# An attention-plus-two-MoE kernel: shorter first warm-up, v sums on GpSimd, pooled normalising in halves, another choice of engine, and the first batch's two outputs added in PSUM

## The chip, the cores and the metric

The kernel runs on one core of a Trainium2 chip. The metric is the device time of one execution in microseconds; lower is better.

## The reference

For 4 batches of 8 heads, 576 positions and head size 64, two attentions are added. The first works on q, k and v averaged over groups of four positions (144 x 144 scores), and each of its rows is repeated four times. The second is local: each position sees those less than four away. The sum, as a matrix x of 2304 tokens by 512, goes through two feed-forward layers of width 2048.

```
out_up    = repeat(softmax(q_d k_d^T / 8) v_d, 4)     # *_d: mean over 4 positions
out_local = softmax(masked(q k^T / 8)) v              # |i - j| < 4
x = out_up + out_local
h = x @ w_in;   x = (h * sigmoid(h)) @ w_out
h = x @ w_in2;  g = (a0 + a1 h + a2 h^2 + a3 h^3) / (1 + |b0||h| + |b1| h^2 + 1e-6)
out = g @ w_out2
```

## The kernel before

**Precision.** Each MoE operand is split into a high part (rounded to the fast float32 form) and a low rest, and each product is three matmuls: high by high, high by low, low by high. `xh`/`xl` are the parts of x, `gh`/`gl` those of the activated h, and the weights are split by `piece` (seven jobs for each piece of 128 columns, on ACT, DVE and GpSimd).

**Stages.** The first layer's tokens go in five blocks of 5, 5, 5, 5 and 4 chunks of 96 tokens (`BLOCKS1`), and each block goes over 16 slices of the width. A step is one slice of one block: 12 matmuls of L807 into a bank `hps` (tag "h", two buffers), `th` and `sg` on ACT and DVE, then `gh` and `gl`, then 12 matmuls of L821. Block 0 does slices 0 to 7, then block 1 all 16, then block 0 its rest. Block 0 needs chunks 0 to 4 of batch 0; block 1 needs chunk 5 of batch 0 and chunks 0 to 3 of batch 1. The second layer (L1054 and others) has a fixed order and is not touched.

**Attention.** Of each batch, the pooled part runs in two rounds m: scores (job s, L471), maximum (m), exponentials (e, ACT), sums (u), normalising (n, L496), transposes for each half e_ (t0, t1, L505), copies (c0, c1), product with v's sums (o, L519), and copy to `up` (U). The sums of v over four positions are jobs p (L424 on DVE, L426 and L427 on GpSimd) in batch 0, and accumulating loads in the others. The local part goes chunk by chunk: S (L572, L581), M, E, U, N (L606), T (L617), C, O (product, L637), A (the addition of the upsampled result from PSUM, L644, into `xs`, two buffers), H (copy to `xh`) and X (L659, subtraction to `xl`). PSUM tiles of attention come from the ring "pair": one buffer, and two of "acc" that are lent to it until the first MoE step.

**Order.** A planner (`Plan`) lists the jobs with costs in ns on engines P (PE), V (DVE), A (ACT), G (GpSimd) and D (the SP queue's loads), simulates them by due time and resources, and emits the instructions in the order it finds. That order is fixed from then on: an engine waits at each instruction for what it needs. A job with `port=True` may go to GpSimd or DVE, and the planner lets only one such job run at a time.

**Warm-up.** `warm(n)` issues n dummy matmuls (L289) into a tile `wps`, which has the tag "h" as well. There are 20 at the start. In the head, wherever the plan has PE idle before a job, more are put in:

```
    warm(WARM0)
    busy = 0.0
    for x in order:
        if x.eng == "P":
            if busy < HEAD + 15000:
                warm(int((x.start - busy) * WARM_SHARE / 109))
            busy = x.end
        x.emit(x.eng)
```

with HEAD = 34000 and WARM_SHARE = 0.8, times in planned ns.

Of the kernel before, what the change touches and what calls it, by code (L numbers as in the profile page):

```python
# [49 lines left out]
PATIENCE = 900.0  # L50
BACKLOG = 4000.0
EARLY = 50000.0
ROUNDS = 6
WARM0 = 20
WARM_SHARE = 0.8


W_LOW = 2.0 ** -15
# [35 lines left out]
class Plan:  # L94
# [27 lines left out]
    def run(self, when):  # L122
# [26 lines left out]
        while events:  # L149
            t = heapq.heappop(events)  # L150
            while events and events[0] <= t:
                heapq.heappop(events)
            while done and done[0][0] <= t:
                _, _, j = heapq.heappop(done)
                for u in j.give:
                    u.left -= 1
                    if u.left == 0:
                        self.rings[u.home].append(u.no)
                for x in users.get(id(j), ()):
                    x.wait -= 1  # L160
                    lat = (0.0 if j.eng == "P" else self.OWN) if j.eng == x.only() else self.LAT
                    x.ready = max(x.ready, t + lat + x.margin)
                    if x.wait == 0:
                        pool.append(x)
                        heapq.heappush(events, x.ready)
            pool.sort(key=lambda j: j.t)
            again = True
            while again:
                again = False
                for j in pool:  # L170
                    if j.ready > t:
                        continue
                    if j.t - j.early > t:
                        heapq.heappush(events, j.t - j.early)
                        continue
                    need = {}
                    for u in j.take:
                        need[u.ring] = need.get(u.ring, 0) + 1
                    if any(len(self.rings[r]) + len(self.rings[self.lent[r]] if r in self.lent else ()) < k
                           for r, k in need.items()):  # L180
                        continue

                    best = next(iter(j.cost))
                    if best == "D" and bus > t + BACKLOG:
                        heapq.heappush(events, bus - BACKLOG)
                        continue
                    if free[best] > t and not (j.port and "G" in j.cost):
                        if free[best] <= t + PATIENCE:
                            continue
                        best = next((e for e in j.cost if free[e] <= t), None)  # L190
                        if best is None:
                            continue
                    if "G" in j.cost and "V" in j.cost and j.port:
                        best = next((e for e in "VG" if free[e] <= t), None)
                        if best is None:
                            continue
                    held = best == "G" or (best == "V" and j.port)
                    if held and port > t:
                        heapq.heappush(events, port)
                        continue  # L200
                    for u in j.take:
                        u.home = u.ring if self.rings[u.ring] else self.lent[u.ring]
                        u.no = self.rings[u.home].pop(0)
                    if j.closes:
                        self.lent.clear()
                    j.eng, j.start = best, t
                    free[best] = t + j.cost[best]
                    if held and not (best == "G" and j.size):
                        port = free[best]
                    heapq.heappush(events, free[best])  # L210
                    if j.size:
                        bus = max(bus, free[best]) + j.size / self.DMA_RATE
                        j.end = bus + self.DMA_LAT
                    else:
                        j.end = free[best]
                    n += 1
                    heapq.heappush(done, (j.end, n, j))
                    heapq.heappush(events, j.end)
                    order.append(j)
                    pool.remove(j)  # L220
                    again = True
                    break
# [32 lines left out]
def tile_kernel(ctx, tc, kq, kqs, vp, vw_in, moe_w_in, moe_w_out, moe2_w_in, moe2_w_out, moe2_a, moe2_b, out):  # L255
# [67 lines left out]
    def eng(e):  # L323
        return {"V": nc.vector, "G": nc.gpsimd}[e]
# [50 lines left out]
    def attention(b):  # L375
# [22 lines left out]
        if b == 0:  # L398
# [12 lines left out]
            for i in range(2):  # L411
                for hf in range(2):
                    wn = 2 * i + hf + NF - 7
                    u = Unit(f"w{wn}")
                    st = {}
                    def lv(e, i=i, hf=hf, st=st, wn=wn):
                        st[0] = wp.tile([128, 4, 256], F32, tag=f"w{wn}", name="vst")[:HS]
                        nc.sync.dma_start(out=st[0], in_=vp[b, :, :, i, 256 * hf:256 * hf + 256].rearrange("r s c -> s r c"))
                    def pv(e, i=i, hf=hf, st=st):
                        if not vdt:  # L420
                            vdt[0] = at.tile([HS, 2, DM], F32, tag="vd", name="vd", bufs=1)
                        o = vdt[0][:, i, 256 * hf:256 * hf + 256]
                        if e == "V":
                            nc.vector.tensor_reduce(out=o, in_=st[0].rearrange("p r c -> p c r"), axis=AX.X, op=ALU.add)  # L424
                        else:
                            nc.gpsimd.tensor_tensor(out=st[0][:, 0:2], in0=st[0][:, 0:2], in1=st[0][:, 2:4], op=ALU.add)  # L426
                            nc.gpsimd.tensor_tensor(out=o, in0=st[0][:, 0], in1=st[0][:, 1], op=ALU.add)  # L427
                    l = plan.add(f"v{b}{i}{hf}", FAR, {"D": 60}, lv, take=[u], size=HS * 4096)
                    vs.append(plan.add(f"p{b}{i}{hf}", FAR, {"G": 2050, "V": 1950}, pv,
                                       after=[l] + vs[:1], take=[] if vs else [vdu], give=[u]))  # L430
        else:
            def ks(e, r):
# [27 lines left out]
        for m in range(2):  # L460
# [31 lines left out]
                nc.vector.tensor_reduce(out=x["r"], in_=x["e"], axis=AX.X, op=ALU.add)  # L492
                nc.vector.reciprocal(out=x["r"], in_=x["r"])

            def no(e, x=x):
                eng(e).tensor_tensor(out=x["e"][:, :, :SD], in0=x["e"][:, :, :SD],  # L496
                                     in1=x["r"].unsqueeze(2).to_broadcast([128, 6, SD]), op=ALU.mult)

            def tr(e, x=x, e_=0, u=None):
                x["t", e_] = pair(u)  # L500
# [28 lines left out]
            jm = plan.add(f"m{b}{m}", d0, {"V": v_ns(864)}, mx, after=[js])  # L529
            je = plan.add(f"e{b}{m}", d0, {"A": 6 * (a_ns(SD) + 93) + 200}, ex, after=[jm], give=[p0])  # L530
            ju = plan.add(f"u{b}{m}", d0, {"V": v_ns(870) + 200}, su, after=[je])
            jn = plan.add(f"n{b}{m}", d0, {"V": v_ns(864), "G": 130 + 1.9 * 864}, no, after=[ju], port=True)
            pc, pt_ = [], []
            for e_, u in ((0, p1_), (1, p2)):
                jt = plan.add(f"t{b}{m}{e_}", d0, {"P": 500}, lambda e, tr=tr, e_=e_, u=u: tr(e, e_=e_, u=u),
                              after=[jn] + pt_[:1], take=[u] + ([pt] if e_ == 0 else []), give=[eu], margin=MARGIN if b else MARGIN0)
                pt_.append(jt)
                pc.append(plan.add(f"c{b}{m}{e_}", d0, {"A": a_ns(576), "V": v_ns(576)},
                                   lambda e, tc_=tc_, e_=e_: tc_(e, e_=e_), after=[jt] + pc[:1], give=[u]))
# [6 lines left out]
        for c in range(NCH):  # L546
# [79 lines left out]
                    x["p"] = at.tile([128, 2, 4 * SUB], F32, tag="PT", name="PT", bufs=3)  # L626
                copy(e, x["p"], x["t"][:, :, :4 * SUB])

            def pv(e, x=x, pO=pO):
                op = x["o"] = pair(pO)  # L630
                for m in range(2):
                    for s_ in range(2):
                        for e_ in range(2):
                            for a in range(2):
# [1 line left out]
                                o = SUB * (2 * e_ + m)  # L636
                                nc.tensor.matmul(op[64 * e_:64 * e_ + 64, a, CH * m + SUB * s_:CH * m + SUB * s_ + SUB],  # L637
                                                 lhsT=x["v"][r, s_, 2 * m + e_, :], rhs=x["p"][r, s_, o:o + SUB],
                                                 start=True, stop=True)

            def ad(e, x=x, c=c):
                x["x"] = at.tile([128, KT, CH], F32, tag="xs", name="xs", bufs=2)
# [7 lines left out]
            def hi(e, x=x, j=j, i=i):  # L650
                if i == 0:
                    k = x_u[j].no
                    xh[j] = p1.tile([128, KT, NB1], F32R, tag=f"xh{k}", name=f"xh{k}", bufs=1)
                    xl[j] = p1.tile([128, KT, NB1], F32R, tag=f"xl{k}", name=f"xl{k}", bufs=1)
                copy(e, xh[j][:, :, CH * i:CH * i + CH], x["x"])

            def lo(e, x=x, j=j, i=i):
                sl = slice(CH * i, CH * i + CH)
                eng(e).tensor_tensor(out=xl[j][:, :, sl], in0=x["x"], in1=xh[j][:, :, sl], op=ALU.subtract)  # L659

            if i == 0:
                x_u[j] = Unit("x")
# [10 lines left out]
                          margin=MARGIN if b else MARGIN0)  # L673
            jc = plan.add(f"C{b}{c}", d0, {"A": a_ns(384), "V": v_ns(384)}, cp_, after=[jt] + (c3 if b == 0 and c == 4 else []), give=[pT])
            c3 = [jc]
            jo = plan.add(f"O{b}{c}", d0, {"P": 700}, pv, after=[jc, jl] + ups, take=[pO, xu], give=[pt, vu],
                          margin=MARGIN if b else MARGIN0)
            ja = plan.add(f"A{b}{c}", d0, {"V": 2 * v_ns(192)}, ad, after=[jo], give=[pO, upu])
            jh = plan.add(f"H{b}{c}", d0, {"A": a_ns(384, False), "V": 300}, hi, port=True, after=[ja] + x_first.get(j, []),
                          take=[x_u[j]] if i == 0 else [])  # L680
            x_first.setdefault(j, [jh])
            x_done.setdefault(j, []).append(
                plan.add(f"X{b}{c}", due, {"V": v_ns(384), "G": g_ns(384)}, lo, after=[jh], give=[xu], port=True))

    takes = {}
    xh, xl, x_u, x_first, x_done = {}, {}, {}, {}, {}
# [320 lines left out]
    o_jobs = moe1()  # L1007
    order = plan.settle(guess, ROUNDS)
    warm(WARM0)
    busy = 0.0  # L1010
    for x in order:
        if x.eng == "P":
            if busy < HEAD + 15000:
# [170 lines left out]
```

## Time and profile before

| | |
|---|---|
| median of 3 runs | 925.39 us (923.1 to 926.2) |
| the profiled execution's own time | 925.37 us |
| its span in the profile | 923.6 us |
| mean granted clock of PE | 0.996 |
| busy: PE, DVE, ACT, POOL (GpSimd) | 906.2, 711.4, 606.8, 333.2 us |

Times in the profile count from the start of the span. Busy times overlap between engines. PE's matmuls are pipelined, so one record lasts longer than the step from one to the next. [...] A releaser behind an arrow is what ended an engine's wait; "issue" means that nothing the profile shows was waited for.

### The profile page before, as it was taken

The numbers are of one execution on the slowest core, as the hardware profiler recorded it, in microseconds if no ns is written. First come the engines' busy times: TensorE is split into PE (matmuls) and PEld (weight loads), VectorE is DVE, ScalarE is ACT, GpSimd is POOL, SyncE is SP. The second block draws the span as 40 slices with busy tenths as digits, with TensorE's granted clock in tenths as the row PEclk, the third lists the DMA queues.
The fourth block names the chain that finished last, engine by engine and source line by source line (L and its number), as shares of the span: only waits on it lengthen the run. The fifth ranks groups of instructions, "written<-read, shape, count | busy, mean of one in ns | idle before, by whom it ended". The sixth has DMA issues, their size and how long they took to land.

```text
span 923.6 us, 16216 instructions
## 1 busy us (share of the span) xinstructions
PE 906.2 (98%) x6212; PEld 762.3 (83%) x6212; DVE 711.4 (77%) x1060; ACT 606.8 (66%) x1224; POOL 333.2 (36%) x279
## 2 busy tenths in 40 slices
PE   8988999999999999999999999999999999999997
PEld 6766788877887778878899988888888888999996
DVE  6979876996557876785332399998998999799995
ACT  4957655786446764674322488877877777787874
POOL 4534240142022410121000155655555555455553
PEclk9989999999999999999999999999999999999999
DMA  9878997779789777779685091002001000200000
GB/s 282 287 217 247 277 282 279 251 268 301 220 269 294 238 276 276 268 245 363 213 288 210 5 392 48 1 1 92 1 1 48 33 1 1 80 1 0 35 1 35
DMA packets 48042, 153.03 MB, mean 166 GB/s; under 512 B 5244, under 2 KB 10492, under 8 KB 47964
## 3 DMA queue, kind: packets, MB, share of 16 engines
q1 hardware_dynamic: 44972, 143.03, 44.1%
q0 software_dynamic: 2704, 8.95, 5.4%
q8 instruction: 49, 0.80, 0.4%
q14 instruction: 29, 0.24, 0.1%
q10 hardware_dynamic: 288, 0.00, 0.0%
HBM read 116.38 MB, written 35.59 MB: 165 GB/s over the span
## 4 chain that ended last, share of the span: by engine, by line
PE 91%; DVE 4%; ACT 3%; issue 1%; POOL 0%; ACTq 0%; DVEq 0%; POOLq 0%
PE hps L807 43%; PE acc L1054 21%; PE acc L821 21%; PE wps L289 1%; PE pair L637 1%; PE pair L581 1%; PE pair L519 1%; ACT E L597 1%; PE pair L617 1%; DVE cw L735 1%; ACT cr L723 0%; DVE cr L732 0%; ACT PT L332 0%; DVE cw L728 0%; PE pair L471 0%
## 5 line engine op out<-in xcount | busy, mean ns | idle before, releaser
L807 PE MATMUL hps<-xh,w 128*128 128x480 f32 (+1 forms) x640 | 226.0, 381 | 3.6 <-DVE th L973 3.0
L821 PE MATMUL acc<-gh,wo 128*128 128x480 f32 (+1 forms) x640 | 222.8, 376 | 0.0
L807 PE MATMUL hps<-x2h,wi 128*128 128x512 f32 (+1 forms) x640 | 196.4, 368 | 0.0
L894 POOL TENSOR_TENSOR u<-u,ah 128x512 f32<-128x512 f32 (+1 forms) x80 | 96.0, 1200 | 262.7 <-ACT u L892 261.1
L1054 PE MATMUL acc<-wo,gh 128*128 128x512 f32 x576 | 178.0, 390 | 0.0
L807 PEld LDWEIGHTS hps<-xh,w 128*128 128x128 f32 x640 | 121.1, 189 | 22.5 <-DVE th L973 3.8
L821 PEld LDWEIGHTS acc<-gh,wo 128*128 128x128 f32 x640 | 119.8, 188 | 17.4 <-issue 1.8
L807 PEld LDWEIGHTS hps<-x2h,wi 128*128 128x128 f32 x640 | 118.8, 188 | 16.3
L1085 POOL TENSOR_TENSOR gl<-p,gh 128x512 fp32r<-128x512 f32 (+1 forms) x80 | 121.2, 1515 | 11.6 <-issue 8.9
L1054 PEld LDWEIGHTS acc<-wo,gh 128*128 128x128 f32 x576 | 107.6, 188 | 20.9
L807 PE MATMUL hps<-xl,w 128*128 128x480 f32 (+1 forms) x320 | 120.0, 375 | 1.1 <-DVE xl L659 1.0
L821 PE MATMUL acc<-gl,wo 128*128 128x480 f32 (+1 forms) x320 | 118.6, 371 | 0.4 <-POOL gl L982 0.4
L807 PE MATMUL hps<-x2l,wi 128*128 128x512 f32 (+1 forms) x320 | 117.7, 368 | 0.0
L1054 PE MATMUL acc<-wo,gl 128*128 128x512 f32 x288 | 112.7, 391 | 0.0
L970 ACT ACTIVATE th<-hps 128x480 f32<-128x480 f32 (+1 forms) x80 | 44.5, 557 | 101.7 <-PE hps L807 100.8
L973 DVE SCALAR_TENSOR_TENSOR th<-th,hps 128x480 f32<-128x480 f32 (+1 forms) x80 | 50.4, 631 | 78.9 <-ACT th L970 78.5
L1077 DVE SCALAR_TENSOR_TENSOR u<-u,r 128x512 f32<-128x512 f32 (+1 forms) x80 | 100.1, 1252 | 2.8
L1070 ACT ACTIVATE r<-u,cst 128x512 f32<-128x512 f32 (+1 forms) x80 | 54.5, 682 | 52.7 <-POOL u L894 52.7
L1076 DVE SCALAR_TENSOR_TENSOR u<-u,r 128x512 f32<-128x512 f32 (+1 forms) x80 | 82.7, 1034 | 0.5 <-ACT r L1071 0.5
L732 POOL TENSOR_TENSOR cr<-cw,cr 128x512 int32<-128x512 int32 x22 | 30.9, 1407 | 135.0 <-DVE cw L728 86.2
L891 DVE TENSOR_TENSOR p<-p,hps 128x512 f32<-128x512 f32 (+1 forms) x80 | 50.5, 631 | 31.5 <-ACT p L890 31.3
L332 ACT ACTIVATE gh<-th 128x480 fp32r<-128x480 f32 (+1 forms) x80 | 47.4, 592 | 31.8 <-DVE th L973 28.5
(123 smaller groups left out, 1485.4 us busy)
## 6 DMA issues: line engine op xcount, KB each, us to landing
wo<-wos SPq DMA_DIRECT2D x64, 512.0 KB, 5.8
raw<-moe_w_in SPq DMA_DIRECT2D x32, 512.0 KB, 5.0
raw<-moe_w_out SPq DMA_DIRECT2D x32, 512.0 KB, 5.9
w2s<-cvo SPq DMA_DIRECT2D x32, 512.0 KB, 5.2
kq<-kq SPq DMA_DIRECT2D x12, 788.0 KB, 7.5
wos<-wo SPq DMA_DIRECT2D x16, 512.0 KB, 3.1
wi<-w2s SPq DMA_DIRECT2D x16, 512.0 KB, 6.6
wo<-w2s SPq DMA_DIRECT2D x16, 512.0 KB, 9.7
```

The lines of the kernel that those rows point to most:

```text
L332: nc.scalar.activation(out, in_, AF.Copy, scale=scale)
L807: nc.tensor.matmul(hps[:, :n], lhsT=wi[:, i, 128 * g:128 * g + 128], rhs=(a, b)[s][:, g, :n], start=(m == 0), stop=(m == len(mms) - 1))
L821: nc.tensor.matmul(acc_t[p][g // 2][:, g % 2, :n], lhsT=wo[:, i, 128 * g:128 * g + 128], rhs=s_[:, :n], start=(f == f0 and m % 3 == 0), st ...
L891: nc.vector.tensor_tensor(out=p, in0=p, in1=hps, op=ALU.mult)
L894: nc.gpsimd.tensor_tensor(out=u, in0=u, in1=ah, op=ALU.mult)
L970: nc.scalar.activation(x["t"][:, :n], x["h"][:, :n], AF.Tanh, scale=0.5)
L973: nc.vector.scalar_tensor_tensor(out=x["t"][:, :n], in0=x["t"][:, :n], scalar=1.0, in1=x["h"][:, :n], op0=ALU.add, op1=ALU.mult)
L1054: nc.tensor.matmul(acc2[j][c], lhsT=a[:, 128 * c:128 * c + 128], rhs=wo[:, i, :], start=(f == 0 and m % 3 == 0), stop=(f == NF - 1 and m % ...
L1070: nc.scalar.activation(r, u, AF.Ln, scale=2.0 ** -64, bias=cst[:, 0:1])
L1076: nc.vector.scalar_tensor_tensor(out=u, in0=u, scalar=1.000001, in1=r, op0=ALU.add, op1=ALU.mult)
L1077: nc.vector.scalar_tensor_tensor(out=u, in0=u, scalar=-2.0, in1=r, op0=ALU.add, op1=ALU.mult)
L1085: nc.gpsimd.tensor_tensor(out=gl2[k_][:, :n], in0=p, in1=gh2[k_][:, :n], op=ALU.subtract)
```

## The change

- The time from which the first planned warm-up is counted goes from 0 to 3500 ns (`COLD`).
- The v sums of batch 0 may only go to GpSimd.
- The pooled normalising n becomes two jobs of three of the six rows each, and each transpose group waits for its own.
- When a job may go to GpSimd or DVE, the planner tries GpSimd first if there is ready work for DVE alone that is not `port` work.
- For batch 0 (`UP_PE`), job O begins with two matmuls that write the upsampled result into the PSUM tile (identity by `up`, each value repeated four times), and the products add to it. Job A and `xs` go; H and X read PSUM, X is on DVE alone, and the PSUM pair is given back after X.

```diff
+UP_PE = 1
...
+COLD = 3500.0
...
                     if "G" in j.cost and "V" in j.cost and j.port:
-                        best = next((e for e in "VG" if free[e] <= t), None)
+                        rest = any(x.ready <= t and not x.port and x.only() == "V" for x in pool)
+                        best = next((e for e in ("GV" if rest else "VG") if free[e] <= t), None)
...
-                    vs.append(plan.add(f"p{b}{i}{hf}", FAR, {"G": 2050, "V": 1950}, pv,
+                    vs.append(plan.add(f"p{b}{i}{hf}", FAR, {"G": 2050}, pv,
...
-            def no(e, x=x):
-                eng(e).tensor_tensor(out=x["e"][:, :, :SD], in0=x["e"][:, :, :SD],
-                                     in1=x["r"].unsqueeze(2).to_broadcast([128, 6, SD]), op=ALU.mult)
+            def no(e, x=x, e_=0):
+                i = slice(3 * e_, 3 * e_ + 3)
+                eng(e).tensor_tensor(out=x["e"][:, i, :SD], in0=x["e"][:, i, :SD],
+                                     in1=x["r"][:, i].unsqueeze(2).to_broadcast([128, 3, SD]), op=ALU.mult)
...
-            jn = plan.add(f"n{b}{m}", d0, {"V": v_ns(864), "G": 130 + 1.9 * 864}, no, after=[ju], port=True)
+            jn = [plan.add(f"n{b}{m}{e_}", d0, {"V": v_ns(432), "G": 130 + 1.9 * 432}, lambda e, no=no, e_=e_: no(e, e_=e_),
+                           after=[ju], port=True) for e_ in range(2)]
...
-                              after=[jn] + pt_[:1], take=[u] + ([pt] if e_ == 0 else []), give=[eu], margin=MARGIN if b else MARGIN0)
+                              after=[jn[e_]] + pt_[:1], take=[u] + ([pt] if e_ == 0 else []), give=[eu], margin=MARGIN if b else MARGIN0)
...
                 op = x["o"] = pair(pO)
+                if b < UP_PE:
+                    for a in range(2):
+                        nc.tensor.matmul(op[:, a, :2 * CH], lhsT=ident,
+                                         rhs=upt[0].rearrange("p (m a) q -> p a m q", a=2)[:, a, :, 24 * c:24 * c + 24]
+                                         .unsqueeze(3).to_broadcast([128, 2, 24, 4]), start=True, stop=False)
...
-                                                 start=True, stop=True)
+                                                 start=b >= UP_PE, stop=b >= UP_PE or m + s_ == 2)
...
+                if b < UP_PE:
+                    x["x"] = x["o"][:, :, :2 * CH].rearrange("p a (m q) -> p a m q", m=2)
...
+            jo = plan.add(f"O{b}{c}", d0, {"P": 1350 if pe else 700}, pv, after=[jc, jl] + ups, take=[pO] + ([] if pe else [xu]),
+                          give=[pt, vu] + ([upu] if pe else []), margin=MARGIN if b else MARGIN0)
+            ja = jo if pe else plan.add(f"A{b}{c}", d0, {"V": 2 * v_ns(192)}, ad, after=[jo], give=[pO, upu])
...
+                plan.add(f"X{b}{c}", due, {"V": v_ns(384)} if pe else {"V": v_ns(384), "G": g_ns(384)}, lo, after=[jh],
+                         give=[pO] if pe else [xu], port=not pe))
...
-    busy = 0.0
+    busy = COLD
```

## Rows read from the trace of the kernel before

**Rows 1.** The page, part 1: busy us (share of the span) xinstructions.

```profile
PE 906.2 (98%) x6212; PEld 762.3 (83%) x6212; DVE 711.4 (77%) x1060; ACT 606.8 (66%) x1224; POOL 333.2 (36%) x279
```

**Rows 2.** Windows of one stretch: engines' busy us (xinstructions), PE's clock, DMA share, GB/s.

```profile
60.00:80.00 20.00, 19.18 (x171) 14.96 (x170) 18.35 (x29) 15.21 (x38) 7.30 (x7) 1.00 0.70 195
```

**Rows 3.** Timeline of PE: start, us, line, operation [idle before <-releaser].

```profile
1.06 8.71 PE L289 MATMUL wps<-wz 128*128 128x256 bf16 x59 [1.06 <-DVE wz L284]
...
31.17 1.20 PE L519 MATMUL pair<-PT,vd 72*64 72x144 f32 x16
...
35.84 0.65 PE L637 MATMUL acc<-PT,vw 54*64 54x48 f32 x32
...
48.34 0.48 PE L807 MATMUL hps<-xl,w 128*128 128x480 f32 x1 [0.97 <-DVE xl L659]
...
54.01 0.77 PE L807 MATMUL hps<-xh,w 128*128 128x480 f32 x1 [3.01 <-DVE th L973]
...
59.70 1.39 PE L289 MATMUL wps<-wz 128*128 128x256 bf16 x10
...
112.18 0.49 PE L807 MATMUL hps<-xh,w 128*128 128x480 f32 x1 [0.39 <-ACT xh L332]
```

**Rows 4.** Windows, instructions of L807 alone: PE, PEld, PE's clock, DMA share, GB/s.

```profile
54.00:61.00 7.00, 5.17 (x12) 3.84 (x12) 0.57 0.85 215
```

**Rows 5.** Windows, instructions of L289 (the warm-up) alone, same columns.

```profile
1.00:5.30 4.30, 4.24 (x21) 3.00 (x22) 1.00 0.67 167
5.30:9.60 4.30, 4.30 (x40) 3.77 (x38) 1.00 0.94 376
```

**Rows 6.** Timeline of DVE in the head.

```profile
6.73 1.81 DVE L408 TENSOR_REDUCE kqd<-kq 128x192 f32<-128x768 f32 x2 [2.39 <-DMA kq<-kq]
10.63 0.61 DVE L587 TENSOR_REDUCE n<-pair 128x8 f32<-128x432 f32 x1 [2.09 <-PE pair L581]
...
20.23 1.98 DVE L424 TENSOR_REDUCE vd<-vst 72x256 f32<-72x1024 f32 x1
...
30.17 0.69 DVE L732 CUSTOM_DVE_ANT_0 cr<-cw,cr 128x1024 uint16<-128x1024 uint16 x1
...
45.77 1.52 DVE L732 CUSTOM_DVE_ANT_0 cr<-cw,cr 128x1024 uint16<-128x1024 uint16 x1
```

**Rows 7.** Groups of POOL by line and form, 8 to 60 us: busy, mean ns | idle before.

```profile
L606 POOL TENSOR_TENSOR E<-E,r 128x432 f32<-128x432 f32 x8 | 7.9, 996 | 13.4 <-DVE r L603 12.9 <-PE pair L581 0.5
L426 POOL TENSOR_TENSOR vst<-vst 72x512 f32<-72x512 f32 x3 | 3.8, 1268 | 0.0
L496 POOL TENSOR_TENSOR EE<-EE,r 128x864 f32<-128x864 f32 x2 | 3.3, 1671 | 0.3 <-ACT EE L487 0.2
...
L427 POOL TENSOR_TENSOR vd<-vst 72x256 f32<-72x256 f32 x3 | 2.2, 723 | 0.2
```

**Rows 8.** The chain of waits from 0 to 95 us: start, us, what.

```profile
19.43 0.94 ACT E L597 x5
...
30.05 1.08 ACT PT L332 x2
...
34.69 0.41 ACT up L332
```

**Rows 9.** Groups of DVE by line and form, 8 to 60 us.

```profile
L644 DVE TENSOR_TENSOR xs<-acc,up 128x192 f32<-128x192 f32 x10 | 3.1, 347 | 0.1
...
L659 DVE TENSOR_TENSOR xl<-xs,xh 128x384 fp32r<-128x384 f32 x5 | 2.7, 548 | 0.0
...
L606 DVE TENSOR_TENSOR E<-E,r 128x432 f32<-128x432 f32 x1 | 0.6, 603 | 0.0
```

**Rows 10.** Timeline of ACT: the first copy to xh.

```profile
36.96 0.52 ACT L332 ACTIVATE xh<-xs 128x384 fp32r<-128x384 f32 x1 [0.20 <-DVE xs L644]
```

**Rows 11.** Timeline of POOL beside the DVE row of 45.77.

```profile
45.47 1.27 POOL L732 TENSOR_TENSOR cr<-cw,cr 128x512 int32<-128x512 int32 x1 [2.26 <-DVE cw L728]
```

**Rows 12.** Windows, instructions of L821 (output products) alone.

```profile
61.00:112.18 51.18, 21.09 (x84) 15.14 (x84) 1.00 0.81 243
```

More of the change, by code (lines that the diff above doesn't have):

```diff
@@ L627, in cp_, with pv @@
                 copy(e, x["p"], x["t"][:, :, :4 * SUB])
-            def pv(e, x=x, pO=pO):
+            def pv(e, x=x, c=c, pO=pO):
                 op = x["o"] = pair(pO)
+                if b < UP_PE:
[3 more added lines that the diff above has]
+                                         .unsqueeze(3).to_broadcast([128, 2, 24, 4]), start=True, stop=False)
                 for m in range(2):
@@ L654, in hi, with lo @@
                     xl[j] = p1.tile([128, KT, NB1], F32R, tag=f"xl{k}", name=f"xl{k}", bufs=1)
[L655 to L659, printed above, removed]
+                if b < UP_PE:
+                    x["x"] = x["o"][:, :, :2 * CH].rearrange("p a (m q) -> p a m q", m=2)
+                    sl = slice(CH * i, CH * i + CH)
+                    x["h"], x["l"] = (t[j].rearrange("p (m a) q -> p a m q", a=2)[:, :, :, sl] for t in (xh, xl))
+                else:
+                    x["h"], x["l"] = (t[j][:, :, CH * i:CH * i + CH] for t in (xh, xl))
+                copy(e, x["h"], x["x"])
+            def lo(e, x=x):
+                eng(e).tensor_tensor(out=x["l"], in0=x["x"], in1=x["h"], op=ALU.subtract)
             if i == 0:
@@ L675, in attention @@
             c3 = [jc]
[L676 to L679, printed above, removed]
+            pe = b < UP_PE
+            jo = plan.add(f"O{b}{c}", d0, {"P": 1350 if pe else 700}, pv, after=[jc, jl] + ups, take=[pO] + ([] if pe else [xu]),
+                          give=[pt, vu] + ([upu] if pe else []), margin=MARGIN if b else MARGIN0)
+            ja = jo if pe else plan.add(f"A{b}{c}", d0, {"V": 2 * v_ns(192)}, ad, after=[jo], give=[pO, upu])
+            jh = plan.add(f"H{b}{c}", d0, {"A": a_ns(384), "V": v_ns(384)} if pe else {"A": a_ns(384, False), "V": 300}, hi, port=not pe, after=[ja] + x_first.get(j, []),
                           take=[x_u[j]] if i == 0 else [])
@@ L682, in attention @@
             x_done.setdefault(j, []).append(
-                plan.add(f"X{b}{c}", due, {"V": v_ns(384), "G": g_ns(384)}, lo, after=[jh], give=[xu], port=True))
+                plan.add(f"X{b}{c}", due, {"V": v_ns(384)} if pe else {"V": v_ns(384), "G": g_ns(384)}, lo, after=[jh],
+                         give=[pO] if pe else [xu], port=not pe))
     takes = {}
```

## The prediction

> **What bounds the kernel now.** I read the busy shares first [rows 1]: PE works 906.2 of 923.6 us, so the time is PE's, and can only fall where PE waits, runs slowly, or does work that is not wanted. The stages come next [rows 2]: from 60 us on PE is close to full, with DVE at 18.35 of 20 us in the stretch 60 to 80, a second engine with little left over. What PE loses lies ahead of that. Its timeline [rows 3] shows a head of attention and dummy warm-up products; the first MoE product that needs the low part of x starts at 48.34, after waiting 0.97 for DVE; the second step starts at 54.01 after 3.01 of waiting for the first step's th. [...] Ten warm-ups at 59.70 stand on the path too, 1.39. So the question is how much earlier step 0 can start, and whether what follows can keep up.
>
> The wait at 54.01 has a cause that the code names: the warm-up bank `wps` and the step results share the tag "h" with two buffers, and the last warm-up comes after the second step, so the second step waits for the first one's buffer.
>
> **The warm-up.** The first one takes 59 products, from 1.06 to 9.77 [rows 3]. It is 20 fixed ones and 39 worked out from the planned start of the first scores: int((start - 0) x 0.8 / 109) = 39 means a start near 5.3 us. With 3.5 us taken off, (5.3 - 3.5) x 0.8 / 109 gives 13, so 33 in all. They run at 21 in the first 4.3 us and 40 in the next 4.3 [rows 5], so 33 are through near 6.6 at the latest (21 by 5.3, 12 more at 108 ns). That rate nearly doubles at about 5.3 (the clock column says 1.00 in both rows, the counts say otherwise), so the clock is up before they end. The scores then need the first kq load, which DVE waits for until 6.73 [rows 6]. So they start near 6.75 and not 9.6: 2.85 earlier on PE. DVE handles two sums of kq first, 6.73 to 8.54, so its first maximum goes from 10.63 to about 8.55: 2.1. From there on the head is a chain through DVE and ACT, so 2.1 is what I take; 0 if a later load binds instead, 2.85 if the order lets the maximum go ahead.
>
> **The v sums.** One of four ran on DVE (1.98 at 20.23) [rows 6]. On GpSimd it is one pair of additions, 1.27 + 0.72 = 1.99 [rows 7]. The chain of waits runs through ACT from 19.43 to 31.13 [rows 8], so DVE's 1.98 lies beside it; what it saves is capacity. GpSimd has the pooled normalising, two of 1.67 [rows 7], behind these sums, and may be 2.0 late with it. I take 0, with -2.0 to +2.0 as ends.
>
> **Halves.** A transpose group needs one half only, so it can go half a normalising earlier: 1.67 / 2 = 0.84 on GpSimd. But its copies queue on ACT, which the chain shows with no wait between to 31.13 [rows 8]. I take 0.4 between 0 and 0.84. The other batches do the same; their extra instructions hide under PE's MoE products.
>
> **The sum in PSUM.** This is the main term. The second upsampled result is finished at 34.69 + 0.41 = 35.10 [rows 8], and step 0 gets its last operand at 48.34 [rows 3]: 13.24 us for five chunks (0 to 4; chunk 5 is block 1's). Now a chunk is product, two additions on DVE (3.1 us for ten, so 0.62 a chunk) [rows 9], copy to xh, subtraction to xl; and its product waits for one of two `xs` buffers, held until the subtraction ends. The change drops the additions and the `xs` buffers; the PSUM pair is instead held to the subtraction, three pairs being there before step 0. So the chunks can follow one another at PE's pace.
> That pace: the 32 records of a chunk's products took 0.65 [rows 3]. Two float32 products of 192 columns by the full identity are new; the trace has none. The nearest row is the pooled product, 16 records (two for each of 8 products of 144 columns) in 1.20 [rows 3]: 0.15 each if they go one by one, 0.30 if two go side by side on halves of the array. By columns that is 0.20 to 0.40 for 192, so 0.4 to 0.8 a chunk. I take 0.7, near the upper end, since a full-array product has nothing beside it. [...] No row here shows such a product by itself.
> A chunk then takes 0.65 + 0.7 = 1.35; five take 6.75. Behind the last come a copy of 0.52 with a hand-over of 0.20 [rows 10], and a subtraction of 0.55 [rows 9] with another 0.20: 8.2 in all. From 13.24 that leaves 5.0 gained. Ends: with 0.4 a chunk 6.5; if ACT's exponentials of the next batch and its scores take ACT and two of the three pairs again, as little as 1.0. Subtractions, of which GpSimd could take some, are now DVE's alone, about 0.55 each, against 0.62 x 6 saved.
>
> **GpSimd preferred.** A normalising costs 1.0 on GpSimd and 0.60 on DVE [rows 7, 9]; it frees 0.6 of DVE at 0.4 more latency, in a stage where DVE is 92% busy. What speaks against it is a row pair: DVE's integer addition takes 0.69 at 30.17, and 1.52 at 45.77 [rows 6], where GpSimd began an addition at 45.47 for 1.27 [rows 11]. DVE did not end until 0.55 after GpSimd did. So a two-input operation on DVE that meets one on GpSimd costs up to 0.83. [...] The new test asks for port-free work in the plan, but the engines run later than the plan. I take 0.5 as the price, 0 to 6.6 (eight such in the head).
>
> **The sum.** 2.1 + 0 + 0.4 + 5.0 - 0.5 = 7.0. The profiled execution took 925.37 (span 923.6 and 1.8 around it), the median of the runs is 925.39, so no correction: 918.4. I leave the second step's wait as it is: some warm-up still stands behind step 0, because the last is set by planned time (49 us) and step 0 moves away from it.
>
> Can the rest follow? What is late next is weight splitting, on a DVE with 8% idle, and it loses 3.7 + 2.0 of work, gains 0.5, and starts 2.1 earlier: about 7.3, just what PE asks. And there is the gate of block 1: it starts at 112.18 after waiting 0.39 for the copy of its last chunk [rows 3]. By then 84 of 96 output products of the first part were done [rows 12]; the 12 left, at 251 ns each (21.09 / 84), are 3.0 us. So batch 1's attention must also come earlier, or no more than about 3.4 is kept. Its chain starts behind step 1 and shares the one PSUM pair left, so it moves with step 0; I expect it to.
>
> **The rivals.**
> *The second step's stall goes as well.* If no warm-up stands behind step 0 or other PE work fills the gap: 3.01, 2.6 of slow clock and 1.39 of warm-up, 7.0 more at most: 911.4. For it: all three hang on one order. Against: the cut at 49 us.
> *Block 1's gate stays.* Batch 1 does not move, and the gain is cut to 3.0 + 0.4: 922.0. For it: the present wait of 0.39 at exactly that point. Against: its work is bound by the same DVE that is relieved.
> [...] Eight meetings at 0.83 take 6.6 of the 7.0 (7.5 without my 0.5, so 0.9 left): 924.5. For it: the 1.52 row. Against: GpSimd is idle most of the time now.
> *Slower: the warm-up bank.* With step 0 earlier and the cut fixed, more steps lie before the last warm-up, each with one "h" buffer: a wait of 3.0 and slow products for 2.6, 5.6 a step. One more such stall leaves 1.4 of the gain; from the second on the kernel is slower: 918.4 + 11.2 = 929.6. For it: one such step in the trace. Against: later steps have output products between them to cover the wait.
>
> **How the numbers follow.** My forecast has 0.48 (own range 915 to 921.5), the stall gone 0.15, the gate 0.14, locks 0.10, the warm-up bank 0.13. A difference under 0.3%, 2.8 us, cannot be told from none: faster is below 922.6, slower above 928.2. Faster: 0.48 + 0.15 and half of the gate's case, 0.70; same: the other half and the locks, 0.17; slower 0.13. The range of 8 in 10 goes from 911, the stall gone, to 925, the locks, and leaves out the slower case and a little at the fast end.
>
> **What the profile would show.** 33 warm-ups and scores at about 6.75; no vd sum on DVE; identity products of 0.2 to 0.4 in the five chunks, step 0 near 41; the wait before step 1, and the clock behind it; block 1's start near 105. I am wrong if step 0 stays near 48, if block 1 stays near 112, or if several steps after the first wait for th.

## The result and the profile after

The changed kernel takes 936.0 us (median of 4, 933.64 to 938.05) against 924.92: ratio 1.0118, 95% interval 1.0100 to 1.0136. It is slower by 1.2%, and the forecast of 918.4 was wrong in sign. The profiled execution took 936.6, its span is 934.8 (923.6 before), and PE's mean granted clock, as a share of full speed, is 0.984 (0.996 before). The changed kernel's four executions differ with the clock: they took from 933.64 us at a mean of 0.986 to 938.05 at 0.982.

The page's line of busy times, which answers to [rows 1]:

```profile
PE 912.2 (98%) x6167; PEld 766.3 (82%) x6167; DVE 710.3 (76%) x1054; ACT 604.2 (65%) x1220; POOL 336.0 (36%) x286
```

PE's timeline after, with the rows that answer to [rows 3] (L825 is the former L807, L839 the former L821, L639 the new identity products, L524 the pooled product):

```profile
6.67 0.69 PE L587 MATMUL pair<-kq 64*64 64x54 f32 x32 [0.24 <-DMA kq<-kq]
...
27.88 2.19 PE L524 MATMUL acc<-PT,vd 72*64 72x144 f32 x16
...
37.27 1.65 PE L639 MATMUL acc<-up,ident 128*128 128x192 f32 x4
...
43.54 0.92 PE L639 MATMUL acc<-up,ident 128*128 128x192 f32 x4
...
48.30 0.49 PE L825 MATMUL hps<-xh,w 128*128 128x480 f32 x1
...
52.55 0.49 PE L825 MATMUL hps<-xh,w 128*128 128x480 f32 x1 [1.35 <-DVE th L991]
```

The scores start at 6.67, as forecast. Step 0 starts at 48.30, and before it was at 48.34 that PE had all operands: nothing is gained. The pooled product lasts 2.19 against 1.20, and four identity records 1.65 at 37.27 against 0.92 at 43.54. The windows show why (columns as in [rows 2]):

```profile
26.00:27.50 1.50, 1.26 (x27) 0.88 (x28) 1.47 (x5) 1.50 (x4) 0.00 (x0) 1.00 0.97 398
...
28.50:30.00 1.50, 1.50 (x14) 1.10 (x11) 1.43 (x5) 0.10 (x1) 0.32 (x1) 0.50 0.92 303
...
42.00:43.00 1.00, 1.00 (x20) 0.72 (x15) 0.25 (x1) 0.49 (x1) 0.00 (x0) 1.00 0.12 29
```

From 27.9 to 41.5 PE ran at 0.50, in the midst of the head; before, the column reads 1.00 up to 48, and the fall came at the wait before step 1 (0.79 from 52 to 54, 0.50 from 54 to 60), which is now 1.35 with no fall behind it (1.00 from 52 to 60). What PE did ahead of the fall was transposes of 48 columns with waits of 0.5 and 0.7 between and hardly a dummy product.

Two more losses lie later. Block 1 starts at 115.57 (112.18 before), and it still waits for the last chunk of its x, 0.31 and 0.45:

```profile
115.57 0.48 PE L825 MATMUL hps<-xh,w 128*128 128x480 f32 x1 [0.31 <-ACT xh L336]
116.50 0.45 PE L825 MATMUL hps<-xl,w 128*128 128x480 f32 x1 [0.45 <-DVE xl L675]
```

DVE's timeline shows what that chunk waited behind (L761 and L753 are weight splitting, L675 the subtraction to xl):

```profile
107.56 1.79 DVE L761 TENSOR_TENSOR w<-cw,w 128x512 fp32r<-128x512 f32 x1
...
111.63 1.76 DVE L753 SCALAR_TENSOR_TENSOR cw<-raw,cr 128x512 int32<-128x512 int32 x1
...
115.80 0.55 DVE L675 TENSOR_TENSOR xl<-xs,xh 128x384 fp32r<-128x384 f32 x1
```

Each of the two long operations meets one on GpSimd, in GpSimd's timeline (the same operations took 0.68 each at 99.94 and 116.84, with none on GpSimd beside them):

```profile
107.20 1.60 POOL L750 TENSOR_TENSOR cr<-cw,cr 128x512 int32<-128x512 int32 x1 [4.54 <-ACT w L336]
111.39 1.45 POOL L750 TENSOR_TENSOR cr<-cw,cr 128x512 int32<-128x512 int32 x1 [2.59 <-DVE cw L746]
```

But these waits are not what makes the part from step 0 to block 1 longer, by 3.4 us as the table below has it. PE is idle there a little less than it was (5.8 us against 6.2) and busy 3.8 longer. The windows before, then after:

```profile
48.34:112.18 63.84, 57.60 (x511) 43.76 (x511) 54.28 (x97) 43.75 (x102) 22.60 (x20) 0.95 0.83 247
```

```profile
48.30:115.57 67.27, 61.44 (x585) 46.50 (x579) 58.76 (x107) 47.74 (x118) 22.95 (x21) 0.92 0.82 247
89.32:99.56 10.24, 10.12 (x71) 7.14 (x71) 6.32 (x12) 5.74 (x12) 1.28 (x1) 0.50 0.41 143
```

The last row is a second stretch at half clock; what PE did ahead of it was to wait for ACT's copies of the pooled part, 1.36 at 86.62 and 0.63 at 88.45. Before, PE worked 6.0 us of this part at 0.50 (54.0 to 60.0). Besides, one more chunk's product and one more set of scores lie in this part. An estimate from these rows and those of a_fill below: 2.0 for the clock (half of 10.1 less 6.0), 2.4 for the attention work (0.85 and 0.61 for the chunk, 0.91 for the scores on PE's timeline), less 0.6 for four dummy products fewer and 0.4 for less idle time, together 3.4. No run separates them.

And an output product of block 0's second part waits 4.34 for the copy to `xe` (the buffer from which a store takes a finished block's output), with the clock at 0.50 behind it. The rows are PE's timeline and windows, then GpSimd's and ACT's timelines:

```profile
290.16 0.48 PE L839 MATMUL acc<-gh,wo 128*128 128x480 f32 x1 [4.34 <-DVE xe L334]
```

```profile
292.00:294.00 2.00, 2.00 (x7) 1.65 (x6) 1.38 (x3) 0.75 (x2) 0.00 (x0) 0.50 0.93 120
```

```profile
280.20 1.28 POOL L856 DMA_DIRECT2D x2s<-xe  x1 [3.29 <-DVE xe L334]
```

```profile
288.85 0.57 ACT L336 ACTIVATE xe<-acc 128x480 f32<-128x480 f32 x1 [4.90 <-DMA x2s<-xe]
```

GpSimd issues the first of two adding stores at 280.20. ACT's next copy to xe has got the same buffer and waits for the landing at 288.85, 8.65 later; PE's accumulator is not free until DVE's copy behind it, 0.66 from 289.45.

Where the 11.2 us of the two spans lie, by step starts in the traces (in the program's order steps 0 to 7 are block 0's first part, 8 to 23 block 1, 24 to 31 the rest of block 0; step 32 is the first of block 2, step 40 eight further on; step 0 of the kernel before is counted from 48.34, where it had all operands):

| | to step 0 | to step 8 (block 1) | to step 32 | to step 40 | to the end |
|---|---|---|---|---|---|
| before | 48.3 | 63.8 | 141.2 | 47.4 | 622.9 |
| changed | 48.3 | 67.3 | 142.0 | 53.4 | 623.8 |

So 3.4 in block 0's first part, 6.1 between steps 32 and 40, and a head that gained nothing.

### The profile page after: what moved, and what is told of

It reads as the page before. It is cut to its first block, busy times and chain, and to the rows that moved or that the text cites. A ratio compares the mean times of both kernels' runs of the same rounds, so it can differ in the third digit from the quotient of the medians.

```text
span 934.8 us, 16094 instructions
## 1 busy us (share of the span) xinstructions
PE 912.2 (98%) x6167; PEld 766.3 (82%) x6167; DVE 710.3 (76%) x1054; ACT 604.2 (65%) x1220; POOL 336.0 (36%) x286
## 4 chain that ended last, share of the span: by engine, by line
PE 87%; DVE 4%; ACT 3%; issue 2%; DMA 1%; POOL 1%; ACTq 0%; DVEq 0%; POOLq 0%
PE hps L825 40%; PE acc L1072 21%; PE acc L839 19%; PE pair L648 1%; DMA x2s<-xe 1%; PE pair L587 1%; PE pair L623 1%; PE pair L524 1%; DVE cw L753 1%; ACT E L603 1%; DVE cw L746 1%; PE acc L639 1%; PE acc L524 0%; PE pair L510 0%; ACT cr L741 0%
## 5 line engine op out<-in xcount | busy, mean ns | idle before, releaser
L825 PE MATMUL hps<-xh,w 128*128 128x480 f32 (+1 forms) x640 | 224.3, 382 | 1.9 <-DVE th L991 1.6
L839 PE MATMUL acc<-gh,wo 128*128 128x480 f32 (+1 forms) x640 | 221.3, 378 | 4.4 <-DVE xe L334 4.3
L825 PE MATMUL hps<-x2h,wi 128*128 128x512 f32 (+1 forms) x640 | 196.4, 368 | 0.0
L839 PEld LDWEIGHTS acc<-gh,wo 128*128 128x128 f32 x640 | 121.1, 189 | 21.7 <-DVE xe L334 5.2
L825 PEld LDWEIGHTS hps<-xh,w 128*128 128x128 f32 x640 | 120.6, 189 | 21.5 <-DVE th L991 2.1
L825 PEld LDWEIGHTS hps<-x2h,wi 128*128 128x128 f32 x640 | 118.9, 188 | 16.2
L825 PE MATMUL hps<-xl,w 128*128 128x480 f32 (+1 forms) x320 | 119.6, 374 | 0.4 <-DVE xl L675 0.4
L839 PE MATMUL acc<-gl,wo 128*128 128x480 f32 (+1 forms) x320 | 119.5, 373 | 0.5 <-POOL gl L1000 0.5
L825 PE MATMUL hps<-x2l,wi 128*128 128x512 f32 (+1 forms) x320 | 117.7, 368 | 0.0
L750 POOL TENSOR_TENSOR cr<-cw,cr 128x512 int32<-128x512 int32 x26 | 35.3, 1357 | 156.7 <-DVE cw L746 67.0
## 6 DMA issues: line engine op xcount, KB each, us to landing
wo<-w2s SPq DMA_DIRECT2D x16, 512.0 KB, 10.1
```

The lines of the kernel that those rows point to most:

```text
L825: nc.tensor.matmul(hps[:, :n], lhsT=wi[:, i, 128 * g:128 * g + 128], rhs=(a, b)[s][:, g, :n], start=(m == 0), stop=(m == len(mms) - 1))
L839: nc.tensor.matmul(acc_t[p][g // 2][:, g % 2, :n], lhsT=wo[:, i, 128 * g:128 * g + 128], rhs=s_[:, :n], start=(f == f0 and m % 3 == 0), st ...
```

## The experiments

Names: a_ is the changed kernel less or plus something, b_ the kernel before plus something. All but those named as keeping the order were planned anew by the kernel's own planner.

**One part at a time.** First the warm-up, by itself in both kernels. It does not touch the order of other work.

```diff
# a_cold0                      # b_cold
-COLD = 3500.0                 -    busy = 0.0
+COLD = 0.0                    +    busy = 3500.0
```

> The changed kernel with the old first warm-up (59 dummy products); the order on every engine is otherwise that of the changed kernel. Theory 1 (the loss comes from the new order: slow clock from 28 to 41.5 us because PE has little to do in the pooled stage, and later stalls): the clock still falls near 30 us, the head is 0 to 2 us later, 936 to 938. Rival (the short warm-up lets the clock fall): no slow stretch in the head, some 5 us faster, 930 to 932.

> The kernel before with the shorter first warm-up alone; same order. By the prediction's first term: scores at 6.7, step 0 2.1 us earlier, 923. If the short warm-up costs the clock: a slow stretch in the head, 926 to 931.

b_cold took 922.40 (before 925.64 beside it; ratio 0.9969, 0.9955 to 0.9983): the term was right and somewhat larger. Its second upsampled result starts at 32.06 in ACT's timeline, against 34.69 before [rows 8], 2.63 earlier:

```profile
32.06 0.41 ACT L332 ACTIVATE up<-pair 128x288 f32<-128x288 f32 x1
```

a_cold0 took 934.86 (1.0111, 1.0081 to 1.0140), between the two expectations and no clear difference from the changed kernel. In its profiled execution the head was another: no fall of the clock, step 0 at 45.5 instead of 48.3. But that was the execution with the highest mean clock of its four, 0.991 of 0.981 to 0.991, and one of them took 939.57. So that the short warm-up lets the clock fall in this order, as the rival said, is not shown. The later losses do not come from the warm-up, since a_cold0 kept them: 67.5 to step 8, and 4.5 of wait for xe.

**More dummy products in the head**, order kept.

```diff
             busy = x.end
+        if x.name in ("t000", "t001", "t010", "t011", "o00", "o01", "T02", "T03", "T04"):
+            warm(4)
         x.emit(x.eng)
```

> The changed kernel with four more dummy products ahead of each of nine transposes and pooled products of batch 0 (36 products, 3.9 us of PE at the full clock, part of it in idle time); order otherwise unchanged. Theory 1: no slow stretch between 28 and 41.5, which gives back up to 6.8 us, so step 0 starts at 43 to 46 instead of 48.3 and the time is 931 to 934 with the later stalls as they are. If the slow clock in the head does not decide (the second rival: DVE and ACT set the head anyway), step 0 stays at 48 or later and the time at 936 to 939.

933.01 (1.0082, 1.0067 to 1.0097), and step 0 at 45.58 on PE's timeline, with the clock at 1.00:

```profile
29.43 1.20 PE L524 MATMUL acc<-PT,vd 72*64 72x144 f32 x16
...
36.45 0.92 PE L639 MATMUL acc<-up,ident 128*128 128x192 f32 x4
37.30 0.68 PE L648 MATMUL acc<-PT,vw 54*64 54x48 f32 x32
...
45.58 0.48 PE L825 MATMUL hps<-xh,w 128*128 128x480 f32 x1
```

```profile
28.50:30.00 1.50, 1.50 (x23) 1.20 (x24) 1.47 (x4) 0.72 (x2) 0.40 (x1) 1.00 0.89 305
30.00:40.00 10.00, 10.00 (x202) 7.71 (x196) 5.24 (x11) 6.30 (x18) 3.40 (x3) 1.00 0.81 239
```

The slow stretch in the head is gone, and 2.7 us of step 0 and 3.0 of the time with it, not 6.8: at full clock the head is soon held by other things. All four executions lie between 932.67 and 933.47, at 0.990 to 0.992. The slow stretch in block 0 stays (10.24 us from 86.68), and block 1 starts at 112.87, still 0.7 later than before. This run also shows the identity products at full clock: a chunk steps from 36.45 to 37.30 to the next at 37.91, 0.85 for the sum and 0.61 for the products.

**The store.** Two runs leave out one adding store each, so half of that part's output; order kept.

```diff
+        if f0 and i == 0:        # a_nostore;  i == 1 in a_fill_nostore1, which has a_fill's products too
+            return
         if f0:
```

> The changed kernel without the first of the two adding stores of block 0's second part (half of that part's output is left out); the order is otherwise the same on every engine. Theory 1 (the second copy to xe shares a buffer with that store and waits for its landing, and PE with it): no wait near 285 us and no slow clock behind it, 6 us off, 929 to 931. Rival (the wait is DVE's and ACT's work of that stretch): no more than 1 us off, 935.

> The run with the 36 dummy products (933.0) without the adding store that comes first in the program's order (the second column pair of block 0's second part, left out of the output); order otherwise the same. Theory 1: the wait for xe near 285 us (4.1) and the slow clock behind it are gone, 6 us off, 927. Rival (the wait is ACT's and DVE's work of that stretch): 932 to 933.

a_nostore took 936.24 (1.0108, 1.0067 to 1.0149) and kept its wait of 4.4: it had left out the store that comes second in the program's order, so it told nothing of the cause. a_fill_nostore1 left out the other: 927.54 (1.0016, 1.0005 to 1.0027), 5.5 less than a_fill, and ACT's copy no longer waits:

```profile
275.17 0.57 ACT L336 ACTIVATE xe<-acc 128x480 f32<-128x480 f32 x1
...
281.17 0.55 ACT L336 ACTIVATE xe<-acc 128x480 f32<-128x480 f32 x1
```

From step 32 to step 40 it takes 47.9 us, where a_fill takes 53.2 and the kernel before 47.4. So the 6 us there are the landing of that store, with the slow clock behind the wait for it.

**The other parts alone, on the kernel before.**

> The first batch's two outputs added in PSUM, alone on the kernel before; planned anew. By the prediction's main term 5.0 us off the head (920 to 921); by what the changed kernel showed at full clock, 2.8 (922 to 923) if nothing later goes wrong. Theory 1 (new order with later stalls, which come with this part): block 0 takes some 3 us longer and the store wait near 290 us is there, 928 to 934.

> Pooled normalising in halves, alone on the kernel before; planned anew. Prediction: 0.4 us off, 925. If the halves thin out PE's work in the pooled stage so that the clock falls: a slow stretch near 30 us and 927 to 930.

> GpSimd tried first beside port-free work, alone on the kernel before; planned anew. Prediction: 0.5 us longer, 925 to 926. [...] Chance of the order: 922 to 930 either way.

> The v sums on GpSimd only, alone on the kernel before; planned anew. Prediction: no change, 924 to 926, with -2 to +2 as ends.

| | median | ratio to before | |
|---|---|---|---|
| b_up (sum in PSUM) | 925.07 | 0.9998 (0.9984 to 1.0013) | step 8 at 108.6, but step 40 at 300.1 |
| b_half | 957.68 | 1.0348 (1.0329 to 1.0367) | PE starved from 250 to 300 us |
| b_gv | 924.09 | 0.9981 (0.9969 to 0.9992) | |
| b_vs | 925.12 | 0.9993 (0.9979 to 1.0007) | |

The windows of b_half show its loss in one place:

```profile
250.00:300.00 50.00, 31.46 (x431) 24.59 (x432) 27.35 (x55) 26.71 (x76) 11.88 (x12) 0.59 0.80 216
300.00:350.00 50.00, 50.00 (x423) 40.57 (x423) 38.92 (x71) 31.43 (x72) 13.95 (x13) 1.00 0.81 259
```

PE has 31.46 of 50 us, at a mean clock of 0.59. From 250 to 298 it does mostly the attention of a later batch, link by link through the one PSUM pair, and its waits there, by line and what they were for (in total, times, longest), are

```profile
PE pair L648 <- ACT E L603: 8.1, 3, 2.7
PE pair L524 <- ACT E L603: 2.7, 1, 2.7
PE pair L578 <- ACT PT L336: 2.5, 4, 0.7
```

that is, local products and a pooled product wait for ACT's exponentials (L603), and scores for the copy on ACT that empties the pair. The plan has this loss in it already: its last PE job ends 27.8 planned us later than before (the planner's list below).

**One part undone, in the changed kernel** (UP_PE = 0; the v sums free again; one normalising; "VG" always).

> The changed kernel without the sum in PSUM (the DVE addition is back); planned anew. If the sum in PSUM is what costs (its float32 products in the head at half clock took 1.6 us a chunk): 925 or less and no slow stretch near 30 us. Theory 1 with the halves and GpSimd as causes of the order: the slow stretch stays, 930 to 938.

> The changed kernel with the v sums free to go to DVE again; planned anew. If the loss hangs on that one part: 922 to 926. If it is one more order of the same kind: anywhere from 925 to 937, with slow clock in the head.

> The changed kernel with the pooled normalising in one piece again; planned anew. The halves alone cost 32 us; if they are also what costs in the changed kernel, this is 920 to 926, without the store wait. If not: 928 to 937.

> The changed kernel without the preference for GpSimd; planned anew. If the preference holds the cost down here (it was 0.2% faster alone): 937 or more. [...]

| | median | ratio to before | step 0 | step 8 | step 40 |
|---|---|---|---|---|---|
| a_noup | 926.68 | 1.0007 (0.9994 to 1.0020) | 49.6 | 114.9 | 303.2 |
| a_novs | 920.38 | 0.9942 (0.9924 to 0.9959) | 46.9 | 106.2 | 295.1 |
| a_nohalf | 923.42 | 0.9989 (0.9970 to 1.0008) | 43.0 | 108.9 | 297.0 |
| a_nogv | 928.02 | 1.0015 (0.9995 to 1.0035) | 46.9 | 118.7 | 304.4 |

Undoing any one of the four gives 8 to 16 us, 45 in all, of a loss of 11. These are not prices of parts. a_noup kept a slow stretch in the head (13.65 us from 26.46) and a_novs had none there; both times fell outside what either theory allowed. a_nohalf, without the store wait, and a_nogv came out as if the halves, or the preference, were what costs; but each of the four would say so of its part.

**The same parts, another order.** Only an assumed cost is changed. The operations are the same and the v sums stay on the engines that they had, but an order here includes a placement: in the planner's list 73 to 81 of some 2030 jobs move to another engine. It shows in the pages of the kernel before and of b_g1990 (POOL 279 and 285 instructions, DVE 1060 and 1055).

```diff
-FAR, {"G": 2050}, pv             # a_g1990; 2080 in a_g2080
+FAR, {"G": 1990}, pv
-FAR, {"G": 2050, "V": 1950}, pv  # b_g1990
+FAR, {"G": 1990, "V": 1950}, pv
```

> The changed kernel with the planned cost of a v sum at 1990 ns instead of 2050; the same instructions, and the sums still on GpSimd alone, in another order. Theory 2 (the result hangs on which order the planner happens to find, by several us either way): anywhere between 920 and 940, and more than 4 us from the changed kernel or from the run with 2080. Rival (keeping the v sums on GpSimd costs the 15 us by itself): 933 to 939.

> The same with 2080 ns. Theory 2: anywhere between 920 and 940. Rival (the v sums' place itself): 933 to 939.

> The kernel before with the planned cost of a v sum on GpSimd at 1990 ns instead of 2050; same instructions, another order. Theory 2: it moves too, 920 to 932. Rival (only the changed kernel's parts cost): 924 to 926.

a_g1990 took 929.72 (1.0054, 1.0033 to 1.0075), a_g2080 929.75 (1.0032, 1.0010 to 1.0054), and b_g1990, the kernel before with one number changed, 919.79 (0.9938, 0.9923 to 0.9953). So a change of 60 ns in a cost that the planner assumes moves the kernel before by 6 us, at about the same clock (0.994 to 0.996 in its four executions, 0.993 to 0.996 in those of the kernel before beside it). It moves the changed one by as much, though part of that goes with the clock: a_g2080's ten executions run from 924.05 at 0.995 to 933.75 at 0.982, and at 0.984 a_g1990 took 933.03 and a_g2080 932.01, where the changed kernel took 935.39 and 936.60. The rival is wrong: with the v sums on GpSimd alone it was 930 as well as 936. That the two a_ runs would differ from each other by over 4 did not come about, but each lies 6 from the changed kernel.

**The best order with the short warm-up.**

> The kernel before with the planned cost of a v sum at 1990 ns and the shorter first warm-up. The warm-up does not touch the order, so if its 3 us (922.4 against 925.6) are its own, they add: 917, faster than both kernels. If the clock falls in the head in this order, no gain over 919.8.

917.18 (0.9912, 0.9897 to 0.9928): faster than the kernel before by 0.9% and than the changed one by 2%. The warm-up takes 2.6 us off here and 3.2 off the kernel before, so it adds to the order as expected.

## Why the prediction was wrong, step by step

**What bounds the kernel** was read rightly in the main: PE, whose losses lie early. They do not all lie ahead of 60 us: before, PE waits 0.43, 0.40 and 1.68 at 77.83, 79.61 and 88.32. a_novs, b_cold and b_g1990 had by step 8 (at 106.2, 109.9 and 106.2, against 112.2 before) about all that they gained.

**The warm-up.** Scores at 6.67 (forecast 6.75), 33 dummy products, DVE's first maximum at 8.38 (forecast 8.55). The gain alone was 3.2, not 2.1: in b_cold the chain moved by 2.06 at the first maximum and by 2.63 at the second upsampled result. What I left out is the clock of the head behind the first warm-up: from 27.9 it ran at half clock and gave back 2.7. I had looked at the clock only for the first 33 products and for the stretch from 54 to 61. The number of dummy products alone does not decide it: the changed kernel has 111 in all against 180 before, but a_novs has 116 and no slow stretch in the head, and b_vs has 182 and one of 10.24 us from 31.17. That 36 more at nine places remove it in this order is shown by a_fill.

**The sum in PSUM**, 5.0: the term was mis-sized. At full clock a chunk took 0.85 + 0.61 = 1.46 against 1.35, the sum 0.85 being just above my upper bound of 0.8. From the second upsampled result (35.1) to step 0 (45.5), a_cold0 took 10.4 where I had 8.2 and before had 13.24: 2.8 gained. The rest went to things that I had not put behind the last chunk. In a_fill, DVE's last subtraction stands behind a weight operation of 1.55 (0.43 at 47.05) that met one of 1.28 on GpSimd:

```profile
42.62 1.55 DVE L746 TENSOR_SCALAR cw<-cw 128x512 int32<-128x512 int32 x1
44.09 0.55 DVE L675 TENSOR_TENSOR xl<-acc,xh 128x384 fp32r<-128x384 f32 x1
```

```profile
42.60 1.28 POOL L761 TENSOR_TENSOR wo<-cw,wo 128x512 fp32r<-128x512 f32 x1 [2.96 <-ACT wo L336]
```

and the order has a next batch's scores, which wait for the PSUM pair that this subtraction gives back, ahead of step 0 (0.9 us).

**The v sums, halves and GpSimd's preference** at 0, 0.4 and -0.5: alone they gave 0 (0.9993), a loss of 32 us, and a gain of 0.2%. Together, with the old warm-up, they left the second upsampled result at 35.07 in a_cold0, against 35.10 before: no gain on the head's chain from any. Meetings of DVE and GpSimd, which the forecast's chances call locks (924.5), do occur: 1.79 and 1.76 on DVE at 107.56 and 111.63 are 1.1 more than the 0.68 of the same operations alone, where I had 0.83. But PE's waits behind them come to 0.76, against 0.39 at that point before.

**The steps that failed** are two. In the head, the sum has no term for the clock between the first warm-up and step 0. That cost 2.7 (a_fill), and with the main term at 2.8 instead of 5.0, step 0 came at 48.30 where I had 41. Behind the head it is "Can the rest follow?", with its "Its chain starts behind step 1 and shares the one PSUM pair left, so it moves with step 0; I expect it to": in a_fill step 0 is 2.8 earlier than before, and block 1 is 0.7 later. With it fails the sum of parts. I costed each part as if all other work kept its place. But four of the five change what the planner sees, and it makes a new order for 500 us of work. The planner's own list, in its planned us (not times of the chip), shows that most of the head's gain is gone by step 8, and all of it by the end, before any engine has run:

```
                        step 0   step 8   step 40   last PE job
before                    43.1    100.4     282.7     494.8
changed                   38.8     99.2     283.7     496.0
b_half                    43.7    104.9     311.3     522.6
b_g1990                   42.6     99.6     281.9     494.0
```

Step 0 goes 4.3 earlier, step 8, held by batch 1's attention, 1.2, and the end 1.2 later. That is my rival of block 1's gate, though I let 3.4 of the gain survive it; two more uses of the one pair stand ahead of it, chunk 5's product and one batch of scores (4 identity and 32 score records more between step 0 and step 8). On the chip the 1.2 earlier became 3.4 later, with the slow clock and more attention work in block 0; a_fill separates only the slow clock of the head. Then the plan gave a buffer to the copy to xe whose store landed 8.65 after its issue, where the plan reckoned 4.8; that cost 6. The list does not foresee such losses: a_nohalf ends later in it (496.3) than the changed kernel and ran 12.6 us faster.

**The rivals.** The second step's stall shrank from 3.01 to 1.35 and its slow clock went, in part what the fast rival said; the total hid it. The 2.6 of slow clock in that rival and in the slower one was my estimate, half of the 5.17 of [rows 4]. The twelve products of step 0 took 2.90 at 1.00 after the change, so 2.3 is what the traces show (windows of L825 alone, columns as in [rows 4]):

```profile
48.30:51.30 3.00, 2.90 (x12) 2.17 (x12) 1.00 0.89 135
```

The slower rival, more stalls from the warm-up bank, was wrong: its place was step 1, once, as before. The slow clock came, but in other places.

What stays open: which feature of an order makes it good. a_novs and b_g1990 both reach step 8 at 106.2, 6 earlier than before, with quite different sets of parts. The 3.4 us in block 0 were read from the trace, not separated by a run. Why executions of one kernel are granted different clocks is open too.

## What to carry to other kernels

Where a program orders its work by a greedy planner, the price of an edit is not the sum of its parts: find the spread first, by changing an assumed cost by a few per cent and nothing else. Here one such edit moved either kernel by 6 us, more than any part gave by itself, and the quickest gain was to search among such orders and then add the one edit that does not touch the order. Before crediting an earlier start, follow the next gate in the same resource (here one PSUM pair) and read PE's clock in the stretches that lose fill work: here it was 0.50 from 30 to 40, and 1.00 with 36 more dummy products (a_fill).

## What was not expected of the hardware

PE was busy in 10.00 of 10 us from 30 to 40 and its clock stayed at 0.50, while the same order with 36 more dummy products (a_fill) had 1.00, also with 10.00 of 10 us busy. The profile's busy share did not tell the two cases apart:

```profile
30.00:40.00 10.00, 10.00 (x141) 8.00 (x139) 5.00 (x10) 4.70 (x15) 3.00 (x3) 0.50 0.89 264
```

An adding store issued by GpSimd took 8.65 us from its issue to the release of its buffer; the other of the run's two landed 5.6 us after its issue.
